# Copying a short filter's result out of PSUM on ScalarE, with the order of a single-core kernel rewritten

## The chip, the cores and the metric

The kernel runs on one core of one Trainium2 chip. The metric is the device time of one execution in microseconds. A core has five engines with a queue each: TensorE (PE, which does the matmuls and writes to PSUM), VectorE (DVE), ScalarE (ACT), GpSimd (POOL) and SyncE (SP, which here only issues DMAs). Each engine executes its own queue strictly in order and waits at an instruction until its inputs are there and its output may be overwritten.

## What is computed

Two long convolutions over a sequence of 2048 positions and 448 channels are mixed with a gate. B stands for the branch with a short shift filter, A for the branch whose kernel comes from a state space model:

```
g = sigmoid((u * gate_w).sum(-1))            # one gate for each position
a = causal_conv(u, K) + u * Dskip            # K from 256 complex modes of each channel
k_shift[t] = sum over 4 taps of k[t - tap] * shift_k[tap]
kv = k_shift * v
b = u * (causal_conv(kv, ssm_k) + kv * ssm_D)
out = g * a + (1 - g) * b
```

The change is at `kv = k_shift * v`, the first thing that branch B needs.

## The kernel before

The 448 channels are worked on in four groups of 112, one for each 32 partitions, and, in time, in four quarters H = 0 to 3 of 28 channels of each group. The list `PLAN` (line 37) names the steps: `T` builds the table of A's kernel for a quarter, `B` and `A` do the convolution of a branch for a quarter, `m` mixes. A convolution spreads its inputs with matmuls (`spread`, line 368), transforms them (`transform`, 380), exchanges halves of the partitions by DMA (`swapped`, 750), multiplies on VectorE (`products`, 426), and goes back by two stages of matmuls (`stage_a`, 397, and `stage_b`, 408). Every result in PSUM must be copied to SBUF by VectorE or ScalarE. A table (`table`, 921) needs exponentials on ScalarE (`exps`, 445), sines (`levels`, 452), a long row of VectorE products (`tables`, 592; three `split`s of each table or half table end in an accumulating DMA issued by GpSimd, line 551) and many small matmuls (`sums`, 632). Quarter 3's table is made in two halves.

Before all that stands a part that is done once: the loads, the constants, the modal part (`Modes.run`, 675: transposes of A, B and C on TensorE, products on VectorE, the copy of B on ScalarE; it fills `hold`, which the exponentials of the first tables read), and the shift filter (line 839). The filter runs over eight blocks of 8 positions of each row; in each, 56 matmuls of k (loaded transposed) with diagonal matrices of the taps (`dg`, 799) fill a PSUM room of 2 x 448 columns, and VectorE multiplies the room with v, in place, in `natv` (line 852).

What sets the order of the work:

- All calls are first recorded and numbered in program order (`Listed`, 112) and then issued in the order of the hand-written list `ORDER` (line 52), which `Order.issue` (132) turns into an order for each engine: each instruction is tied to the one ahead of it on its engine. The profile so shows line 137 for all of them, and they are told apart by tile.
- `SIDES` (45) holds one letter for each copy out of PSUM, phase addition and change of sign (`Sides`, 336): V for VectorE, S for ScalarE.
- `ROOMS` (41) says which of four PSUM rooms (`ps0` to `ps3`) each user takes, `SLOTS` (38) which of seven SBUF buffers (`q0` to `q6`, 3584 columns of bf16) each user takes. The buffers are reused, so a user waits for the one before it. The taps have a buffer of their own call (line 766): their raw form `wr` in the first half, `dg` in the second.

In the trace, `natv` holds v and then kv; `natu` first holds k and then u; `ps` is a PSUM room; `TP` and `TQ` are the table's products; `ET` its exponentials and sines.

Of the kernel before, what the change touches and what calls it, by code (L numbers as in the profile page):

```python
# [38 lines left out]
    "201031456232433120056615532041060303231061540604265013"  # L39
)  # L40
ROOMS = (
    "031230120122130132023010223312031201320001012121201100302332131110331210203301002313130323111031203103303210320132212000"
    "13111112310221033031032020012311212323010303033031323212102022201023121232131202010303130"
)
SIDES = (
    "SVSSSSSVSSSSSSSSSSSSSSSSSSSSSSSVSSSVSSVSSSSSSSSSSSSSSSSSSVVVVVSSSSSSSSSSSSSSSSSSSSSSSSSSSSSSSSSSSSSSSSSSSSSVVVVSSSSSSSSS"
    "SSSSSSSSSSSSSSSSSSSSSSVSSSSSSSSSSSSSSVSVVSVVSSSSSSVSSSSSSSSSSSVSSVVSSSSSSSSSVSVSVSSSVSSS"
)
ORDER = (
# [643 lines left out]
def body(  # L693
# [21 lines left out]
    V = nc.vector  # L715
# [120 lines left out]
    kg = KGen(nc, places, cons, ar, arena, sel_d, d4, hold, evac)  # L836
    nc.gpsimd.memset(shaped(arena["TQ"][:], [32, 2 * M])[:, 31], 0.0)

    for b0 in range(0, 64, 8):
        pt = places.room()  # L840
        for i in range(2):
            for d in (0, -1, 1, -2, 2, -3, 3):
# [170 lines left out]
```

## Time and profile before

| | |
|---|---|
| three timed executions | 260.49, 262.22, 262.29 us (median 262.22) |
| span of the profiled execution (a time of its own beside the span is not on its page) | 257.9 us |
| mean granted clock of TensorE | 0.929 |
| instructions on TensorE, VectorE, ScalarE | 5631, 378, 278 |
| idle time of VectorE behind its last instruction | 10.3 us |

The page's first part gives the busy time of each engine; a view by stretches gives the same between two times, in the order PE, PE's weight loads, DVE, ACT, POOL. The view of waits says who waited for whom: total, times, longest. A group by form is `line engine op out<-in shapes xcount | busy us, mean ns | idle before us`. Instructions of VectorE and ScalarE that follow each other overlap by some 0.08 to 0.15 us in the records, so the time from start to start is a little under the mean.

### The profile page before, as it was taken

The page shows a single profiled execution, that of the slowest core. Times are in us where ns is not written, and L with a number is a line of the kernel's source. Part 1 is how long each engine was busy: PE and PEld are TensorE (multiplying, and loading weights), DVE is VectorE, ACT ScalarE, POOL GpSimd, SP SyncE. Part 2 cuts the span into 40 slices and gives each one's busy share as a digit, 9 for nine tenths or more (in the row PEclk, how much of TensorE's full clock was granted, in tenths as well). Part 3 has the DMA queues.
Part 4 walks back from the last instruction along what each step waited for, and adds up shares of the span by engine and source line. Part 5 has one row for each costly group of instructions (what it writes and reads, how often), then busy time and mean ns, then how long its engine had stood idle before and what let it go on. Part 6 is the DMA issues. An engine that isn't in the chain of part 4 may idle for free.

```text
span 257.9 us, 12431 instructions
## 1 busy us (share of the span) xinstructions
PE 208.9 (81%) x5631; PEld 188.6 (73%) x5631; DVE 237.4 (92%) x378; ACT 199.5 (77%) x278; POOL 30.5 (12%) x81
## 2 busy tenths in 40 slices
PE   0634784988779999998889998989999998999820
PEld 0511484978669898997879887888899897998810
DVE  4999999999999999999999999988999999998830
ACT  2299993089979999999999999989999975653300
POOL 8970001200000002100000021000031120000000
PEclk9995596899979999999999999997999999999975
DMA  6999983499861347475043055600462375120088
GB/s 167 212 164 216 165 178 74 82 171 159 139 157 32 47 106 144 79 167 91 7 99 104 3 102 95 149 24 3 111 110 38 57 145 131 29 51 4 3 163 125
DMA packets 58917, 26.44 MB, mean 103 GB/s; under 512 B 49520, under 2 KB 57200, under 8 KB 58864
## 3 DMA queue, kind: packets, MB, share of 16 engines
q1 hardware_dynamic: 52192, 18.65, 39.5%
q0 software_dynamic: 2160, 5.51, 12.2%
q10 hardware_dynamic: 4512, 1.49, 3.0%
q8 instruction: 44, 0.72, 1.2%
q14 instruction: 9, 0.07, 0.1%
HBM read 8.17 MB, written 2.52 MB: 41 GB/s over the span
## 4 chain that ended last, share of the span: by engine, by line
DVE 61%; PE 17%; issue 6%; DMA 5%; ACT 5%; SPq 1%; POOL 1%; DVEq 0%; ACTq 0%; POOLq 0%
DVE TP L137 18%; PE ps L137 17%; DVE q L137 15%; DVE TQ L137 15%; DVE natv L137 5%; ACT q L137 3%; DMA TP<-TP 3%; DVE ET L137 3%; DVE G L137 2%; DVE RK L137 1%; SPq L137 1%; DMA q<-q 1%; ACT ET L137 1%; DMA sk<-in_B_ssm_k_dram 1%; DVE hold L137 1%
## 5 line engine op out<-in xcount | busy, mean ns | idle before, releaser
L137 ACT CAST q<-ps 128x1024 bf16<-128x1024 f32 (+4 forms) x151 | 126.6, 929 | 23.9 <-PE ps L137 23.1
L137 PEld LDWEIGHTS <-q 128*128 128x128 bf16 (+2 forms) x720 | 52.3, 147 | 13.5 <-DMA q<-in_A_A_re_dram 8.4
L137 DVE TENSOR_TENSOR TQ<-TQ,ET 128x896 bf16<-128x896 bf16 (+2 forms) x70 | 45.5, 687 | 0.1
L137 PEld LDWEIGHTS <-natu 128*32 128x32 bf16 (+1 forms) x560 | 30.6, 183 | 8.9 <-issue 7.2
L137 PE MATMUL ps<-TP,TQ 128*32 128x32 bf16 x1792 | 33.3, 240 | 4.1 <-DVE TQ L137 2.6
L137 PE MATMUL ps<-q,s_W 128*128 128x112 bf16 (+1 forms) x544 | 33.8, 214 | 3.5 <-ACT q L137 3.4
L137 PE MATMUL ps<-sa_R,q 128*128 128x128 bf16 x448 | 33.3, 229 | 2.4 <-DVE q L137 1.0
L137 PEld LDWEIGHTS <-TQ 128*32 128x32 bf16 x1792 | 30.1, 153 | 6.7 <-DVE TQ L137 3.1
L137 DVE TENSOR_TENSOR q<-q,q 128x3584 bf16<-128x3584 bf16 (+1 forms) x22 | 32.4, 1513 | 1.2 <-ACT q L137 1.2
L137 PEld LDWEIGHTS <-s_W 128*128 128x128 bf16 x544 | 28.2, 100 | 6.5 <-issue 4.5
L137 DVE TENSOR_TENSOR TP<-TP,ET 128x1792 bf16<-128x1792 bf16 (+3 forms) x25 | 31.4, 1275 | 0.1
L137 POOL DMA_DIRECT2D TP<-TP x15 | 13.1, 914 | 153.8 <-PE ps L137 89.6
L137 PEld LDWEIGHTS <-G 128*128 128x128 bf16 x1024 | 27.9, 96 | 4.3 <-issue 2.5
L137 PE MATMUL ps<-q,G 128*128 128x28 bf16 x1024 | 28.5, 175 | 1.4 <-ACT q L137 1.4
L137 ACT ACTIVATE q<-hold 128x224 bf16<-128x224 f32 x64 | 22.4, 414 | 5.0 <-DVE hold L137 5.0
L137 PE MATMUL ps<-q,natu 128*32 128x336 bf16 (+3 forms) x336 | 17.8, 334 | 5.7 <-DVE natv L137 4.2
L137 ACT ACTIVATE ET<-q 128x1344 bf16<-128x1344 int16 (+1 forms) x12 | 17.2, 1457 | 1.4 <-DVE q L137 1.3
L137 PE MATMUL ps<-q,q 128*32 128x336 bf16 (+3 forms) x112 | 17.8, 334 | 0.0
L137 PE MATMUL ps<-Wc,natu 128*64 128x128 bf16 x224 | 15.5, 285 | 0.6 <-DVE q L137 0.6
L137 ACT CAST RK<-ps 128x448 bf16<-128x448 f32 (+1 forms) x16 | 11.5, 742 | 5.4 <-PE ps L137 5.4
L137 DVE TENSOR_TENSOR TQ<-TQ 128x448 bf16<-128x448 bf16 (+2 forms) x35 | 15.3, 446 | 0.1
L137 DVE CAST q<-ps 128x1024 bf16<-128x1024 f32 (+3 forms) x13 | 12.6, 978 | 2.4 <-PE ps L137 1.4
(81 smaller groups left out, 276.6 us busy)
## 6 DMA issues: line engine op xcount, KB each, us to landing
q<-q SPq DMA_DIRECT2D x64, 112.0 KB, 3.1
TP<-TP POOLq DMA_DIRECT2D x9, 448.0 KB, 5.0
natv<-in_B_v_dram SPq DMA_DIRECT2D x4, 448.0 KB, 7.3
sk<-in_B_ssm_k_dram SPq DMA_DIRECT2D x16, 112.0 KB, 3.8
natu<-in_A_u_dram SPq DMA_DIRECT2D x4, 448.0 KB, 10.2
TP<-TP POOLq DMA_DIRECT2D x6, 224.0 KB, 3.8
out_dram<-natv SPq DMA_DIRECT2D x8, 112.0 KB, 4.6
out_dram<-natv ACTq DMA_DIRECT2D x8, 112.0 KB, 4.5
```

The source lines that it names most:

```text
L137: ins = f(*args, **kw)
```

## The change

1. In the filter, ScalarE (by the new letters in `SIDES`, S for all eight) copies each block from PSUM to SBUF in bf16, and VectorE's product with v reads that copy. The copies use two buffers in turn, each of 2 x 448 columns, in the half of the taps' buffer that held `wr`, which is spent once `dg` is built. The blocks are recorded in the order 16, 48, 8, 24, 32, 0, 40, 56.
2. `SLOTS`, `ROOMS`, `SIDES` and `ORDER` are written anew. The instructions are otherwise the same.

```
-    for b0 in range(0, 64, 8):
+    for i0, b0 in enumerate((16, 48, 8, 24, 32, 0, 40, 56)):
         pt = places.room()
...
         o = vt[:, b0:b0 + 8].rearrange("p (i b) l -> p i (b l)", i=2)
-        V.tensor_tensor(out=o, in0=pt[:, :, 0:448], in1=o, op=ALU.mult)
+        f = shaped(taps, [2, 448], at=896 * (i0 % 2))
+        evac(f, pt[:, :, 0:448])
+        V.tensor_tensor(out=o, in0=f, in1=o, op=ALU.mult)
```
```
 SLOTS = (
-    "201031456232433120056615532041060303231061540604265013"
+    "020260153465641042231116123354602264421130151001205634"
 )
```

The lists `ROOMS`, `SIDES` and `ORDER` are long strings; what the new ones say, read off by laying the recorded calls of both kernels beside each other:

- Beside the eight new copies on ScalarE, twelve things change sides. To ScalarE go three 1024-wide copies out of PSUM, one 896-wide, one 512-wide, one 448-wide, the 64-wide copy of the gate's sums and one 672-wide phase addition; to VectorE go three 896-wide phase additions and one 448-wide copy. VectorE then has 374 instructions and ScalarE 290 with its DMA issues left out.
- `SLOTS` puts the taps into buffer 0, in which A_re, A_im and B_re were loaded first (before, they had buffer 1 for themselves). The DMA that loads them moves from the first place of ScalarE's queue to the 18th, behind twelve exponentials and the copy of B.
- The two instructions that build `dg` were VectorE's 17th and 22nd and are its 69th and 64th.
- VectorE's first half of `hold` was its 36th instruction and is its 31st. The product for the half that is held back (`xfd`), which stood ahead of it, stands behind it.
- On GpSimd the partition index `c_pidx` comes first, and the four longest fills come behind some forty short ones; before, a long fill came first.
- On SP the four transposed loads of k come ahead of the four loads of v; before, one load of v stood between them.
- Ahead of the first copy of a spread, ScalarE's queue holds 60 instructions where it held 46: added are the eight filter copies, seven exponentials of the second table and one change of sign; one exponential and one phase addition move behind it.
- VectorE's 99th instruction is the last product with v in both orders; ahead of it, seven products and sums of the first table's `TQ` now take the place of two of its three splits, four phases of the second table and a change of sign.
- The steps of the convolutions and tables behind that keep their sequence by and large, and are interleaved anew.

More of the change, by code (lines that the diff above doesn't have):

```diff
@@ L38 @@
 SLOTS = (
-    "201031456232433120056615532041060303231061540604265013"
+    "020260153465641042231116123354602264421130151001205634"
 )
 ROOMS = (
-    "031230120122130132023010223312031201320001012121201100302332131110331210203301002313130323111031203103303210320132212000"
-    "13111112310221033031032020012311212323010303033031323212102022201023121232131202010303130"
+    "02131320012123120310303112130210300312021332031302013210231213011301130113201301221330221123000013133021310132220223"
+    "210023220032132301310012023231122032123303232020211313032101330302333110201302112031131230223"
 )
 SIDES = (
-    "SVSSSSSVSSSSSSSSSSSSSSSSSSSSSSSVSSSVSSVSSSSSSSSSSSSSSSSSSVVVVVSSSSSSSSSSSSSSSSSSSSSSSSSSSSSSSSSSSSSSSSSSSSSVVVVSSSSSSSSS"
-    "SSSSSSSSSSSSSSSSSSSSSSVSSSSSSSSSSSSSSVSVVSVVSSSSSSVSSSSSSSSSSSVSSVVSSSSSSSSSVSVSVSSSVSSS"
+    "SSSSSSSSSSSSSSSSSSSSSSSSSSSSSSSSSSSSSSSSSSSSSVSSSSSSSSSSSSSSSSSSVVVVVVVSSSSSSSSSSSSSSSSSSSSSSSSSSSSSSSSSSSSSSSSSSSVV"
+    "VVVVSSSSSSSSSSSSSSSSSSSSSSSSSSSSSSSSSSSSSVSSSSSSSSVVSSVVSSSSSSVSSSSSSSSSSSSSSSSVSSSSSSSSSVSSSSSVSSVS"
 )
 ORDER = (
[54 rows of a table removed]
[54 rows of a table added]
 )
```

108 rows, old and new, of the table ORDER are left out of this document.

## The prediction

> **What bounds the kernel now.** I read the page's busy shares first, then the busy time of each engine in six stretches, then the waits of ScalarE and TensorE, then single groups by form and stretches of the timeline.
>
> ```profile
> span 257.9 us, 12431 instructions
> PE 208.9 (81%) x5631; PEld 188.6 (73%) x5631; DVE 237.4 (92%) x378; ACT 199.5 (77%) x278; POOL 30.5 (12%) x81
> ```
> ```profile
> 0.00:13.45 13.45, 4.75 (x48) 4.09 (x48) 10.01 (x37) 3.40 (x4) 12.21 (x36) 1.00 0.93 185
> 13.45:40.73 27.28, 15.14 (x240) 9.86 (x241) 27.04 (x49) 27.22 (x44) 4.60 (x29) 0.74 1.08 169
> 40.73:52.48 11.75, 10.26 (x256) 9.23 (x256) 11.75 (x13) 0.09 (x1) 2.74 (x3) 0.73 0.53 100
> 52.48:204.28 151.80, 138.95 (x3799) 129.25 (x3800) 148.44 (x222) 146.60 (x201) 9.25 (x12) 0.98 0.49 91
> 204.28:247.60 43.32, 39.76 (x1292) 36.17 (x1290) 40.09 (x61) 22.20 (x31) 1.72 (x2) 1.00 0.30 64
> 247.60:257.90 10.30, 0.00 (x0) 0.00 (x0) 0.04 (x1) 0.00 (x0) 0.00 (x0) 0.54 0.88 145
> ```
>
> The columns of the second fence are the stretch, its length, and busy time (count) of PE, PE weight loads, DVE, ACT and POOL, then the TensorE clock, the DMA share and GB/s. VectorE (DVE) carries 237.4 of 257.9 us, and of its 20.5 us without work 10.3 lie behind its last instruction, where only stores run. But the share is an average. From 13.45 to 40.73 both VectorE and ScalarE are full. From 40.73 to 52.48 VectorE is full and ScalarE does nothing (0.09 of 11.75). From 52.48 to 204.28 all three are nearly full: of 151.80 us VectorE lacks 3.36, ScalarE 5.20, TensorE 12.85. After that ScalarE has room and VectorE and TensorE (40.1 and 39.8 of 43.3) share the bound.
>
> ```profile
> ACT q L137 <- PE ps L137: 23.1, 14, 11.7
> ACT q L137 <- DVE hold L137: 5.0, 1, 5.0
> PE ps L137 <- DVE natv L137: 5.2, 3, 4.2
> ```
> ```profile
> 40.89 2.08 DVE L137 TENSOR_TENSOR natv<-ps,natv 128x896 bf16<-128x896 f32 x2
> ...
> 52.93 1.08 DVE L137 TENSOR_TENSOR natv<-ps,natv 128x896 bf16<-128x896 f32 x1
> 53.93 0.61 DVE L137 TENSOR_TENSOR TQ<-TQ,ET 128x896 bf16<-128x896 bf16 x1
> ```
>
> The hole in ScalarE has a cause that can be read off: TensorE waited 4.2 us in one piece for a VectorE product to give back a PSUM room, and ScalarE waited 11.7 us for TensorE. The eight products of the filter with v sit in VectorE's queue between 40.9 and 53.9, and nothing of the first convolution can be spread before the rooms are free.
>
> **The change, part by part.** Durations are means by form from the same execution.
>
> ```profile
> L137 DVE TENSOR_TENSOR natv<-ps,natv 128x896 bf16<-128x896 f32 x8 | 8.4, 1079 | 0.0
> L137 DVE TENSOR_TENSOR TQ<-TQ,ET 128x896 bf16<-128x896 bf16 x36 | 21.7, 621 | 0.1
> L137 DVE CAST q<-ps 128x1024 bf16<-128x1024 f32 x6 | 7.3, 1222 | 2.1 <-PE ps L137 1.1 <-ACT ET L137 1.0
> L137 DVE CAST q<-ps 128x896 bf16<-128x896 f32 x2 | 2.2, 1080 | 0.0
> L137 DVE CAST q<-ps 128x512 bf16<-128x512 f32 x2 | 1.4, 691 | 0.3 <-PE ps L137 0.3
> L137 DVE TENSOR_SCALAR q<-q 128x672 int32<-128x672 int32 x6 | 3.5, 592 | 0.1
> L137 DVE COPY gx<-ps 128x64 f32<-128x64 f32 x1 | 0.2, 221 | 0.0
> L137 ACT CAST q<-ps 128x1024 bf16<-128x1024 f32 x64 | 64.0, 1044 | 16.6 <-PE ps L137 16.2 <-DVE TP L137 0.3
> L137 ACT CAST q<-ps 128x512 bf16<-128x512 f32 x20 | 12.4, 622 | 0.6 <-PE ps L137 0.4
> L137 ACT CAST q<-ps 128x896 bf16<-128x896 f32 x58 | 51.9, 951 | 4.3 <-PE ps L137 4.2
> L137 ACT ACTIVATE q<-q,quarter 128x896 int32<-128x896 int32 x4 | 4.2, 1057 | 0.0
> ```
>
> (1) The product. It read PSUM (1079 ns); now both inputs are bf16 in SBUF, the form of the second row (621 ns). That is 8 x 0.458 = 3.66 us off VectorE.
>
> (2) The new letters for who copies. VectorE loses three 1024-wide copies (3.67), one 896-wide (1.08), one 512-wide (0.69) and the small gate copy (0.22). Two 448-wide copies cancel. It gains three 896-wide phase additions and loses one 672-wide: no row shows the 896 form on VectorE, so it is bounded by 592 ns below and by 592 x 896/672 = 789 above; I take 789, since its ns grow with size, which makes 3 x 0.789 - 0.592 = +1.78. VectorE's sum is -3.66 - 3.67 - 1.08 - 0.69 - 0.22 + 1.78 = -7.5 us.
>
> (3) ScalarE gains the eight filter copies, 8 x 0.951 = 7.6, three 1024-wide (3.1), one 896 (0.95), one 512 (0.62), and gives away the three additions (3.2): some 10 us of means. In a row the copies follow each other faster, as the next fence shows: two 896-wide copies start at 68.27 and the next instruction at 69.86, so 0.80 each.
>
> ```profile
> 13.45 0.67 ACT L137 ACTIVATE q<-hold 128x224 bf16<-128x224 f32 x2 [4.98 <-DVE hold L137]
> 15.56 2.90 ACT L137 ACTIVATE q<-hold 128x224 bf16<-128x224 f32 x10
> 52.48 4.94 ACT L137 CAST q<-ps 128x1024 bf16<-128x1024 f32 x5 [11.67 <-PE ps L137]
> 68.27 1.84 ACT L137 CAST q<-ps 128x896 bf16<-128x896 f32 x2
> 69.86 0.54 ACT L137 ACTIVATE q<-hold 128x224 bf16<-128x224 f32 x1
> ```
>
> (4) Does ScalarE reach the first spread copy later? Ahead of it stood 46 instructions, now 60. What is added is eight copies (8 x 0.80 = 6.4), seven exponentials of the second table (10 take 2.90, so 2.0) and a sign change; an addition and an exponential go behind it: +8.0 us net. It used to have all that done by 40.73 and then stood until 52.48. It also starts earlier: its first exponential waited until 13.45 for VectorE's first half of `hold`, which was VectorE's 36th instruction and is now its 31st, ahead of the products for the tables held back, and GpSimd's partition index, the first thing VectorE waits for, is now GpSimd's first instruction and no longer behind a long iota.
>
> ```profile
> 0.84 2.00 POOL TP L137
> ```
> ```profile
> 10.50 1.87 DVE L137 TENSOR_SCALAR one<-TP 128x32 bf16<-128x32 int32 x1
> 12.81 0.61 DVE L137 TENSOR_TENSOR hold<-ps,TP 128x448 f32<-128x448 bf16 x1
> ```
>
> That iota took 2.00 us. Against it, long GpSimd fills now come later, and VectorE stood in one of them (an instruction of 32 columns took 1.87 us at 10.50). I take 2 us earlier, between 0 and 3. The two buffers cost something: copy n+2 waits for product n, and by the order this makes ScalarE wait about 0.8 us in all. So the first spread copy comes at 40.73 + 8.0 - 2.0 + 0.8 = 47.5 instead of 52.48, 5.0 us earlier. VectorE passes the last filter product earlier too: the same number of instructions (99) now holds 4.1 us less work by their own records, so 49.8 for 53.93. TensorE finishes the filter when the copies let it, some 5 us earlier.
>
> (5) From there to the last copy of the second A convolution (204.28) ScalarE has 2.6 us more work than before (added up in the same way, 10.6 more up to that point, 8.0 of them already done). With the waits it had, 5.20 us, it comes there at 204.28 - 5.0 + 2.6 = 201.9, a gain of 2.4. VectorE, with its old waits, gains its whole 7.5. TensorE's work is unchanged; it starts 5 us earlier and has 12.85 us of waits, so it does not forbid 7.5. The gain lies between 2.4 and 7.5. Waits in this stretch are mutual, and an engine that would be 2.6 us late uses up part of its 5.20 us of waits; I take about the middle, 4.8.
>
> (6) Moves that I cost at nothing. The shift taps now live in the buffer of A_re, A_im and B_re, so their load leaves ScalarE's queue not at its start but behind twelve exponentials and the copy of B: 11.45 + 12 x 0.29 + 1.6 = 16.5 us. The taps are first read by VectorE's 64th instruction; the 63 ahead of it hold 24.1 us by their own records, and with the 3 us that VectorE stood before them that is 27. VectorE's modal part so covers the load for 10 us; cover gone, each us is a us of the end. On SP the four transposed loads of k now stand ahead of all loads of v, which is the same issue work in another order: the last load of v leaves near 27, as before (21.80 + 5.14 below), and v is first used past 40. The loads of u, at SP, wait for the filter's last matmul, which comes earlier. On GpSimd the accumulating DMAs keep their places behind VectorE's splits; the tightest, in the last table, has 5.2 us from split to use.
>
> ```profile
> 21.80 5.14 SPq L137 DMA_DIRECT2D natv<-in_B_v_dram x3
> ```
> ```profile
> L137 POOL DMA_DIRECT2D TP<-TP x15 | 13.1, 914 | 153.8 <-PE ps L137 89.6
> ```
> ```profile
> TP<-TP POOLq DMA_DIRECT2D x6, 224.0 KB, 3.8
> natv<-in_B_v_dram SPq DMA_DIRECT2D x4, 448.0 KB, 7.3
> q<-in_B_shift_k_dram ACTq DMA_DIRECT2D x1, 448.0 KB, 5.4
> ```
>
> Those accumulating DMAs take 0.9 us to issue and land after 3.8, so 5.2 is enough with little over.
>
> Sum: span 257.9 - 4.8 = 253.1. The timed median, 262.22, lies 4.3 above that span; I keep that distance, so 257.4 us.
>
> **A rule weighed.** In these rows a copy and a product cost 951 + 621 = 1572 ns against 1079. The Trainium skill, "VectorE: DVE Perf Modes", section "Rules for kernel authors", says that an elementwise operation on a matmul's output should either accept the slow rate or be copied to SBUF first if many operations follow; here only one follows, so the rule speaks against this change. By it the sum would be a loss of eight times 0.49 us of engine work; by the rows the two halves are on different engines, and one of them is in an 11.7 us hole. What it would give as a mechanism is rival A.
>
> **Rivals.**
> A. ScalarE becomes the pace and gives it all back. For it: 146.6 of 151.8 us are full and 2.6 are added. Then the earlier start of `hold` does not come (first spread copy at 49.5, 3.0 earlier) and the waits stay: 262.22 - 3.0 + 2.6 = 261.8, no measurable change. Against it: waits of 5.2 us are there to shrink.
> B. The taps land late; this is the one that ends slower. VectorE executes in order, so it stands at its 64th instruction, and filter, copies and spread with it. Break-even is a landing at 27 + 4.8 = 31.8 us; beyond 34.4 it is over 1% slower. For it: the load now falls into the stretch with a DMA share of 1.08, until 40.7 us. The worst I can argue is a landing with the old stretch's last loads, near 36.5: 257.4 + 9.5 = 266.9. Against it: v's loads of the same size in that stretch took 7.3 us, which makes 24. The Trainium skill, "DMA: Bandwidth & Descriptors", has each DMA engine take turns between queues; by that rule a load on ScalarE's own queue does not stand behind SP's and B does not happen, but no row here shows the two at once.
> C. The rewritten order brings waits of its own past 52 us, where three engines are 92 to 98% full. One place decides: the last table's splits. If their DMA needs more than 5.2 us, VectorE and then the last sums wait, in each half of that table; to lose 4.8 + 2.6 us and be 1% slower it must land 3.7 us later both times, 8.9 us behind its split where the rows give 4.7. That gives 264.8 and, at double the rows' 4.7, 266.
> D. All of VectorE's 7.5 us is got: 254.7. This is the good end of the forecast.
>
> **How the numbers follow.** Two runs of this kernel differ by up to 0.7%, so about 1% (2.6 us) is what a measurement can tell from none. Forecast with D (254 to 259.6): 0.60. A and its neighbours (259.6 to 264.8): 0.18. B: 0.11. C: 0.11. So faster 0.60, same 0.18, slower 0.22; the time is the forecast's, 257.4. The forecast's own range is 254.0 to 259.6. For 8 in 10 the range must take in A and half of B and C: 254.0 to 266.0, which leaves out about 0.1 above and 0.1 below.
>
> **What would show it.** VectorE's busy sum near 230 with 374 instructions, the product near 620 ns; ScalarE near 208; ScalarE's first spread copy near 47.5 and no wait above 4 us between 14 and 47 (step 4); VectorE's 64th instruction without idle before it (B wrong) or with a wait for the DMA of B_shift_k (B right); ScalarE's last copy of the second A convolution between 197 and 202 (step 5), or at 204 and later (A); no wait of VectorE for the TP accumulation (C wrong). The prediction is wrong if ScalarE's hole is filled and the end does not move, or if VectorE's idle time grows by more than 7.5 us.

## The result and the profile after

The changed kernel took 259.75 us (median of 19 executions, 257.51 to 261.93), the kernel before, beside it on the same chip, 260.61. The ratio is 0.9932 (95% interval 0.9902 to 0.9961), so 1.8 us were gained, and I had forecast 4.8. (The ratio leaves out executions more than 1.5% above the fastest of their kernel, three of the 19 after and one of the 19 before; with them the two medians lie only 0.9 us apart.) A second measurement of the same two kernels gave 0.9962 (0.9930 to 0.9993), or 1.0 us. The gain is real and small. The time lies inside my range of 254.0 to 266.0, but just outside the forecast's own 254.0 to 259.6, beside rival A's "no measurable change". The profiled execution has a span of 258.0 us against 257.9 before.

The page of the changed kernel, first its busy sums, then the stretches shown above (columns: stretch, length, PE, weight loads, DVE, ACT, POOL, TensorE clock, DMA share, GB/s):

```profile
span 258.0 us, 12418 instructions
PE 205.7 (80%) x5631; PEld 187.0 (72%) x5631; DVE 233.3 (90%) x374; ACT 208.2 (81%) x290; POOL 31.0 (12%) x81
```
```profile
13.45:40.73 27.28, 14.86 (x192) 8.72 (x196) 27.28 (x40) 21.15 (x24) 4.31 (x8) 0.94 1.08 172
40.73:52.48 11.75, 10.45 (x340) 9.99 (x334) 11.75 (x20) 10.67 (x22) 1.50 (x2) 1.00 0.40 76
52.48:204.28 151.80, 137.13 (x3831) 128.90 (x3832) 145.60 (x216) 145.19 (x198) 10.17 (x12) 0.99 0.47 92
204.28:247.60 43.32, 38.27 (x1248) 34.95 (x1237) 38.23 (x60) 22.29 (x30) 2.87 (x4) 0.96 0.33 70
```

ScalarE's hole from 40.73 to 52.48 is filled, as the change meant (0.09 us of work before, 10.67 now). But a new hole has come ahead of it: from 13.45 to 40.73 ScalarE works 21.15 of 27.28 us, where it worked 27.22. The timeline of ScalarE in the changed kernel shows where (the number in brackets is the idle time ahead of the row, and who ended it):

```profile
7.75 3.19 ACT L137 ACTIVATE q<-hold 128x224 bf16<-128x224 f32 x11 [0.81 <-DVE hold L137]
...
17.74 0.86 ACT L137 ACTIVATE q<-q,quarter 128x672 int32<-128x672 int32 x1 [4.71 <-POOL natu L137]
...
37.04 0.91 ACT L137 CAST q<-ps 128x896 bf16<-128x896 f32 x1 [1.74 <-PE ps L137]
...
44.63 1.71 ACT L137 CAST q<-ps 128x896 bf16<-128x896 f32 x2 [0.74 <-DVE natv L137]
46.69 0.91 ACT L137 CAST q<-ps 128x896 bf16<-128x896 f32 x1 [0.34 <-DVE natv L137]
```

ScalarE starts 5.70 us earlier than before (7.75 for 13.45), then stands 4.71 us. The row names GpSimd, but what it waits for is the phases that VectorE makes for it: it starts 0.09 us behind the seventh of eight operations, which ends at 17.65. VectorE's own timeline shows them:

```profile
9.74 0.62 DVE L137 TENSOR_TENSOR hold<-ps,TP 128x448 f32<-128x448 bf16 x1
10.40 7.53 DVE L137 TENSOR_SCALAR q<-hold 128x224 int32<-128x224 f32 x8
17.85 0.60 DVE L137 TENSOR_TENSOR q<-ps,TP 128x448 f32<-128x448 bf16 x1
```

Eight operations on 224 columns, 7.53 us. The group that holds them was cheap before and is not now (kernel before, then the changed one):

```profile
L137 DVE TENSOR_SCALAR q<-hold 128x224 int32<-128x224 f32 x40 | 10.1, 298 | 0.2
```
```profile
L137 DVE TENSOR_SCALAR q<-hold 128x224 int32<-128x224 f32 x40 | 14.8, 421 | 2.8 <-ACT ET L137 2.7
```

The 4.7 us more are busy time, not idle time: VectorE counts as working. Beside it, at those times, GpSimd makes the long fills of the sine tables, which the new order had moved behind some forty short instructions. Two of the fills, and VectorE's operations over the same time, in narrow stretches of the timeline:

```profile
12.29 1.98 POOL L137 IOTA TP<- 32x2048 bf16 x1
14.55 1.81 POOL L137 MEMSET TP<- 32x2048 bf16 x1
```
```profile
11.90 2.50 DVE L137 TENSOR_SCALAR q<-hold 128x224 int32<-128x224 f32 x2
14.33 2.17 DVE L137 TENSOR_SCALAR q<-hold 128x224 int32<-128x224 f32 x2
```

The fills end at 14.27 and 16.36, VectorE's pairs at 14.40 and 16.50: the first pair's second operation (12.30 to 14.40) and the second pair's (14.54 to 16.49) stand until a fill is done. Taken one by one, all eight operations end 0.13 to 0.14 us behind some instruction of GpSimd: three behind a long fill, the others behind short ones of 0.16 to 0.66 us. ScalarE's last filter copy and its first spread copy share a row:

```profile
49.95 1.82 ACT L137 CAST q<-ps 128x896 bf16<-128x896 f32 x2
```

A spread copy takes 1.02 us and the pair ends at 51.77, so the first spread copy comes at 50.75, not at my 47.5. A second new wait lies at 67 us, where ScalarE stands for the gate's matmuls, and these for the load of u (views of waits):

```profile
ACT gx L137 <- PE ps L137: 4.1, 1, 4.1
```
```profile
PE ps L137 <- DMA natu<-in_A_u_dram: 3.1, 1, 3.1
```

### The profile page after: what moved, and what is told of

It is laid out like the page before. It is cut to its first block, busy times and chain, and to the rows that moved or that the text cites. A ratio compares the mean times of both kernels' runs of the same rounds, so it can differ in the third digit from the quotient of the medians.

```text
span 258.0 us, 12418 instructions
## 1 busy us (share of the span) xinstructions
PE 205.7 (80%) x5631; PEld 187.0 (72%) x5631; DVE 233.3 (90%) x374; ACT 208.2 (81%) x290; POOL 31.0 (12%) x81
## 4 chain that ended last, share of the span: by engine, by line
PE 34%; ACT 26%; DVE 17%; DMA 9%; issue 6%; SPq 3%; ACTq 0%; DVEq 0%
PE ps L137 34%; ACT q L137 22%; DVE q L137 6%; DMA natu<-in_A_u_dram 5%; DVE TP L137 5%; SPq L137 3%; DMA q<-in_A_A_re_dram 2%; DMA q<-q 2%; ACT ET L137 2%; DVE G L137 1%; ACT RK L137 1%; DVE ET L137 1%; DVE RK L137 1%; DVE natv L137 1%; ACT L137 1%
## 5 line engine op out<-in xcount | busy, mean ns | idle before, releaser
L137 ACT CAST q<-ps 128x896 bf16<-128x896 f32 (+4 forms) x165 | 137.9, 927 | 18.3 <-PE ps L137 17.0
L137 PEld LDWEIGHTS <-q 128*128 128x128 bf16 (+2 forms) x720 | 51.5, 147 | 14.1 <-issue 6.3
L137 PE MATMUL ps<-q,s_W 128*128 128x112 bf16 (+1 forms) x544 | 32.8, 211 | 6.1 <-ACT q L137 5.4
L137 PEld LDWEIGHTS <-s_W 128*128 128x128 bf16 x544 | 27.4, 98 | 8.5 <-issue 6.8
L137 PEld LDWEIGHTS <-natu 128*32 128x32 bf16 (+1 forms) x560 | 27.9, 181 | 4.8 <-issue 4.4
L137 DVE TENSOR_SCALAR q<-hold 128x224 int32<-128x224 f32 x40 | 14.8, 421 | 2.8 <-ACT ET L137 2.7
L137 PE MATMUL ps<-q,q 128*32 128x336 bf16 (+3 forms) x112 | 15.0, 300 | 2.6 <-DVE q L137 2.6
L137 PE MATMUL ps<-TP 128*128 128x512 bf16 x16 | 7.8, 614 | 10.7 <-POOL TP L137 5.1
L137 PE MATMUL ps<-Wc,natv 128*64 128x128 bf16 x224 | 15.0, 284 | 1.3 <-DVE natv L137 0.9
L137 PE MATMUL ps<-q,natu 128*32 128x336 bf16 (+3 forms) x336 | 15.4, 301 | 0.5 <-DVE q L137 0.4
```

Of the source, the lines that this page charges most:

```text
L137: ins = f(*args, **kw)
```

## The experiments

Two theories stood against each other. The theory of the two waits: the forecast's mechanism holds, and its start was lost first to the fills and then to u. The rival, pace: from 52 us on three nearly full engines set the time, and an earlier start is swallowed. Ratios are to the kernel before, measured beside each. The numbers in the edits are those of the recorded calls.

**The changed kernel again** (no edit).

> The changed kernel once more, unaltered, as the yardstick for the kernels beside it. Both theories: a ratio to the kernel before of about 0.993, ScalarE's first spread copy near 50.75, ScalarE standing some 4 us near 67 for the gate's matmuls.

Measured 0.9962 (0.9930 to 0.9993). It is the yardstick for the next three, which ran beside it.

**The fills moved.** 80 to 83 are the four fills, 110, 112, 113 and 119 phases and a mask, 79 the product that makes `Wc`, 195 a sum of the modal part.

```
 ORDER, the calls of GpSimd alone:
-... 91 118 6 26 ... 18 17 83 21 25 30 28 80 90 81 40 82 89 85 39
+... 91 118 81 83 6 26 ... 18 17 21 25 30 28 90 89 85 80 82 40 39
 ORDER, the calls of VectorE alone:
-... 156 110 119 79 112 113 203 ... 195 199 ...
+... 156 203 ... 195 110 119 79 112 113 199 ...
```

> The four long GpSimd fills of the sine tables (2.0, 2.0, 1.8, 1.8 us) are put elsewhere in GpSimd's order: two where VectorE waits for the first half of hold, two under VectorE's PSUM sums; five short VectorE operations that nobody needs early go behind those sums. Nothing else changes. Theory of the two waits (the early start was lost first to these fills, then to the wait for u): the eight operations that took 7.53 us take about 2.5, VectorE's busy time falls from 233 to about 229, ScalarE's first spread copy comes near 46.5 instead of 50.75, and the end comes 2 to 3.5 us sooner than in the changed kernel: ratio to the kernel before 0.980 to 0.986. Rival (three full engines set the pace from 52 to 204 us and swallow any earlier start): the first spread copy comes just as early, but the end stays within 0.8 us of the changed kernel: ratio 0.990 to 0.996.

Measured 0.9784 (0.9732 to 0.9835), 4.7 us less than the yardstick: the rival's value is outside the interval, and the gain is even a little above the theory's. VectorE, GpSimd and ScalarE in this kernel:

```profile
9.26 1.90 DVE L139 TENSOR_SCALAR q<-hold 128x224 int32<-128x224 f32 x8
...
13.71 3.94 DVE L139 TENSOR_TENSOR TP<-ps,RK 128x1792 f32<-128x1792 bf16 x2
```
```profile
9.53 5.96 POOL L139 IOTA TP<- 128x6 int32 x26
15.53 1.80 POOL L139 MEMSET TP<- 32x2048 bf16 x1
```
```profile
45.41 2.02 ACT L139 CAST q<-ps 128x896 bf16<-128x896 f32 x2 [0.43 <-PE ps L139]
```

The eight operations take 1.90 us for 7.53. The fill at 15.53 now runs wholly under VectorE's two sums from PSUM, and they take 3.94 us, exactly as without a fill beside them in the changed kernel (20.11, 3.94). The first spread copy starts at 46.42: 4.35 us earlier than the yardstick's 50.77. So the shift reached the end in full. The run moves five operations of VectorE too, so the 4.35 us are not those of the eight alone; that the fills are what held the eight is shown by 1.90 for 7.53.

**The gate from v.** The gate's matmuls read v in the place of u, so that nothing there waits for u; the gate that comes out is not the one of the function.

```
-                         rhs=uu[:, :, l], ...
+                         rhs=vt[:, :, l], ...
```

> The gate's 112 matmuls read v in the place of u, so the gate is computed from the wrong tensor, and nothing there waits for the load of u, which is still made. Theory of the two waits: TensorE's 3.1 us for u and ScalarE's 4.1 us for the gate go, the stretch from 64 to 72 us closes up, and the end comes 2 to 4 us sooner than in the changed kernel: ratio 0.978 to 0.986. Rival (pace): the 4 us come back as other waits behind 72 us, ratio 0.990 to 0.996.

Measured 0.9944 (0.9912 to 0.9976): no gain that can be told from the yardstick. Here the theory of the two waits fails in its second half. The wait for u is gone, and two things take its place. VectorE still waits for the next load of the same queue, the second block of `ssm_k` (yardstick, then this kernel):

```profile
71.54 0.29 DVE L137 TENSOR_TENSOR sk<-sk,dB 128x28 bf16<-128x28 bf16 x1 [1.94 <-DMA sk<-in_B_ssm_k_dram]
```
```profile
71.07 0.28 DVE L137 TENSOR_TENSOR sk<-sk,dB 128x28 bf16<-128x28 bf16 x1 [1.47 <-DMA sk<-in_B_ssm_k_dram]
```

And TensorE, which then has the table's sums to do without a pause, stands four times between its own matmuls with nothing that the profile shows to wait for ("issue"):

```profile
75.54 0.32 PE L137 MATMUL ps<-TP,TQ 128*32 128x32 bf16 x7 [1.14 <-issue]
...
79.82 1.22 PE L137 MATMUL ps<-TP,TQ 128*32 128x32 bf16 x63 [0.74 <-issue]
...
83.55 0.33 PE L137 MATMUL ps<-TP,TQ 128*32 128x32 bf16 x7 [0.98 <-issue]
...
87.46 1.15 PE L137 MATMUL ps<-TP,TQ 128*32 128x32 bf16 x57 [0.55 <-issue]
```

That is 3.41 us from 70 to 92; the yardstick has 0.29 there, in one place. TensorE also waits 1.7 us for VectorE's addition on ssm_k there. That these waits are what took the gain back is read from the timeline; no run takes them away. Laid instruction by instruction beside the yardstick, ScalarE is 1.8 us ahead at 80 us and level with it at 88.

**Both together** (the edits of the last two).

> The moved fills and the gate from v together (the gate is again computed from the wrong tensor). Theory of the two waits: the gains add, 4 to 7 us sooner than the changed kernel, ratio 0.966 to 0.978, the first spread copy near 46.5. Rival (pace): ratio 0.988 to 0.995, with the waits of ScalarE and VectorE behind 80 us longer by what the front gained.

Measured 0.9759 (0.9704 to 0.9815): the moved fills' gain, and nothing beyond it that the interval shows. The rival's value is ruled out. The theory's range holds 0.9759 too, but only because the fills alone gave more than it expected; the second gain, which was to be added, is not there.

**The copies undone.** The changed kernel's order, with the product reading PSUM as before the change; `evac.vector()` only passes over the letter in `SIDES`, and the calls are renumbered, since eight fall away.

```
-        f = shaped(taps, [2, 448], at=896 * (i0 % 2))
-        evac(f, pt[:, :, 0:448])
-        V.tensor_tensor(out=o, in0=f, in1=o, op=ALU.mult)
+        evac.vector()
+        V.tensor_tensor(out=o, in0=pt[:, :, 0:448], in1=o, op=ALU.mult)
```

> The changed kernel with its order, but the eight products read PSUM again and the eight ScalarE copies are gone. Theory (the copies carry filter work into ScalarE's hole, and what the first spread copy gains or loses goes through to the end almost whole): VectorE spends 8 x 0.45 = 3.6 us more by its last filter product, ScalarE's first spread copy comes at 53 to 54.5 instead of 50.75, ScalarE's busy time falls by 7.5 us, and the end is 2.5 to 4 us later than in the changed kernel: ratio to the kernel before 1.004 to 1.012. Rival (what the changed kernel gained came from its order alone, and ScalarE is the pace): 7.5 us less work on ScalarE make it no slower than the changed kernel, ratio 0.985 to 0.998.

Measured 1.0148 (1.0101 to 1.0194), some 4.9 us slower than the yardstick by the two ratios (5.7 against 0.9932) and a little more than the theory expected. The first spread copy comes 4.9 us late, more than the products' 3.7 alone; VectorE also waits 2.7 us for the filter's matmuls:

```profile
55.68 1.01 ACT L138 CAST q<-ps 128x1024 bf16<-128x1024 f32 x1 [14.36 <-PE ps L138]
```

So the change of the code is worth about 5 us in this order, which was written for it, and ScalarE, relieved of 6 us, is not the pace.

**Fills moved and copies undone.**

> The moved fills, and the products read PSUM again without the copies. Theory: 2.5 to 4 us later than with the moved fills alone (0.978), ratio 0.988 to 0.995. Rival (ScalarE is the pace): no later than with the moved fills alone, 0.972 to 0.982.

Measured 0.9843 (0.9770 to 0.9916) from executions that scatter over 7 us. It lies between the two and on the edge of both. In its one profile (span 260.5, for 255.5 with the fills moved alone) the first spread copy starts at 51.31 and the two pairs of the table below at 98.99 and 220.34, which is 4.9, 4.7 and 4.6 us later. That is the theory's direction and the size of the run before; by the times, 1.5 us, how much the copies are worth once the fills are moved stays open.

**Three copies back to VectorE**, on top of the moved fills.

```
 SIDES: letters 39, 46 and 150
-S S S
+V V V
```

> The moved fills, and three large PSUM copies given back to VectorE, as the kernel before had them (one 896-wide near 68 us, two 1024-wide near 71 and 164 us): ScalarE is relieved of 2.9 us, VectorE gets 3.5 us more. Theory (neither engine alone sets the pace, their waits are mutual): within 1 us of the moved fills alone, ratio 0.974 to 0.982. Rival A (ScalarE is the pace): 1.5 to 2.9 us sooner, 0.967 to 0.973. The opposite (VectorE is still the pace): 2 to 3.5 us later, 0.986 to 0.992.

Measured 0.9959 (0.9916 to 1.0001): 4.6 us slower than the moved fills alone by the ratios, worse than all three expected and nearest to the opposite (VectorE is still the pace). VectorE now waits at two of the copies:

```profile
67.38 1.09 DVE L139 CAST q<-ps 128x896 bf16<-128x896 f32 x1 [4.66 <-PE ps L139]
```
```profile
165.50 1.23 DVE L139 CAST q<-ps 128x1024 bf16<-128x1024 f32 x1 [2.70 <-PE ps L139]
```

At 67 us VectorE now stands at a copy whose matmuls are behind the gate's, in the wait for u, with all of the tables queued behind it, and 98 us later once more. But these waits stand in the place of others (with the moved fills alone VectorE waits 2.95 us at 67 us for ssm_k). In the two profiles VectorE stands idle for 28.0 us without these copies and 27.8 with them; its busy sum is 2.6 us larger (230.1 for 227.5) and the span 2.4 us longer (257.9 for 255.5). So in the profiles the copies cost what they add to VectorE's work, which speaks for VectorE as the pace. Why the times differ by more stays open.

**Two transforms ahead of the gate's matmuls**, alone and with the moved fills.

```
 ORDER:
-697-760 2044 1629 761-808 1648-1655 1554 872 1630-1637 809 875 1656 ... 1638
+2044 1629 1648-1655 1630-1637 697-808 1554 872 1656 1638 809 875 ...
```

> The changed kernel with the fills where they are, and only the two transforms put ahead of the gate's matmuls on TensorE (their two copies ahead of the gate's copy on ScalarE). Theory (a shift that exists at 88 us is carried unchanged to the end, so what the stretch from 64 to 72 us loses counts): 1.3 to 2.2 us sooner than the changed kernel, ratio to the kernel before 0.986 to 0.992. Rival (as the gate from v suggested, the time comes back as gaps between TensorE's matmuls before 88 us): no gain, ratio 0.992 to 0.997.

> The moved fills, and on TensorE two transforms (with their two copies on ScalarE) ahead of the gate's matmuls, so that ScalarE has 1.6 us of work while u lands. Theory after the gate from v changed nothing (behind u stands the load of the second ssm_k block, and it is this row of loads that holds the stretch): no change, ratio 0.975 to 0.982. Rival (ScalarE's 4.5 us of waiting at the gate are lost at the end): 1.3 to 1.8 us sooner, 0.970 to 0.974.

> The moved fills with the two transforms ahead of the gate once more, unaltered, to compare with the kernels beside it. Both theories: a ratio to the kernel before of 0.970 to 0.977.

Alone: 0.9921 (0.9881 to 0.9962), on the border of the two expectations and not to be told from 0.9932 and 0.9962. With the moved fills: 0.9735 (0.9687 to 0.9783) and, measured once more, 0.9766 (0.9705 to 0.9827), against 0.9784 for the fills alone. What this adds is less than can be told. It is the fastest version measured, 2.3 to 2.7% below the kernel before.

**VectorE's addition on ssm_k later**, on top of that.

```
 ORDER:
-... 879 1853-1869 1905-1912 868 877 ...
+... 879 868 877 1853-1869 1905-1912 ...
```

> The moved fills, the two transforms ahead of the gate, and VectorE's small addition on the second ssm_k block behind a 2.0 us product instead of ahead of it, since VectorE stood 2.4 us there. Theory (VectorE's position past 72 us goes through to the end): VectorE's wait falls from 2.4 to under 1 us, 1 to 2 us sooner than without this move, ratio 0.965 to 0.970. Rival (TensorE and ScalarE wait for u and set the position at 72 us): no change, 0.971 to 0.977.

Measured 0.9804 (0.9738 to 0.9870), no better than 0.9766 beside it: no gain, as the rival said. But the move did not do what the theory needs. In this run's profile VectorE still stands 1.90 us at the addition, now at 70 us, and then 1.65 us at the next copy out of PSUM, so the wait was moved rather than taken away; what it is worth is not shown.

**GpSimd's old order** in the changed kernel.

```
 ORDER, the calls of GpSimd alone:
-1 225 109 223 214 63 75 2 20 ... 83 ... 80 90 81 ... 82 89 85
+81 1 2 5 31 63 225 75 109 15 20 83 6 ... 82 ... 80 ...
```

> The changed kernel with GpSimd's first 55 instructions in the sequence of the kernel before (the long fills at 0.8, 4.3, 6.8 and 10.4 us again, the partition index behind the first); all other engines keep the changed order. Theory of the fills: the first half of hold comes 3 to 5 us later than 7.1, the level operations meet only one fill instead of four, and the first spread copy comes between 48.5 and 51.5; the end within 2 us of the changed kernel, ratio 0.985 to 1.002. Rival (the early partition index is what brought the gain and the late fills cost nothing): the first spread copy at 53 or later and the end 2 us or more later than in the changed kernel, 1.003 or more.

Measured 1.0122 (1.0067 to 1.0177): the rival's case, and I had the size of the first term wrong. The first five rows below are VectorE's, the last is ScalarE's:

```profile
4.40 1.73 DVE L139 TENSOR_SCALAR TP<-TP 128x1 f32<-128x1 int32 x2
...
6.70 1.86 DVE L139 TENSOR_SCALAR TP<-TP 128x32 int32<-128x32 int32 x2 [0.34 <-POOL TP L139]
10.16 2.08 DVE L139 TENSOR_SCALAR gx<-TP 128x128 f32<-128x128 int32 x1 [1.60 <-POOL TP L139]
...
15.29 0.62 DVE L139 TENSOR_TENSOR hold<-ps,TP 128x448 f32<-128x448 bf16 x1 [1.46 <-ACT TP L139]
...
17.76 1.80 DVE L139 TENSOR_SCALAR q<-hold 128x224 int32<-128x224 f32 x8
```
```profile
52.52 2.02 ACT L139 CAST q<-ps 128x896 bf16<-128x896 f32 x2 [0.43 <-PE ps L139]
```

The level operations are quick (1.80 us) because the fills are over, but `hold` comes 8.2 us later than 7.09. The late index is only a part of that (VectorE waits 3.06 us for it at the start, for 1.00 in the changed kernel): three of the fills now stand over VectorE's first small operations, up to 6.13, 8.56 and 12.24 us. So the old place of the fills is not free either, and what the index alone is worth is not shown. Both together: against the old order of GpSimd the new one gains 4 to 5 us (1.0122 against 0.9932 and 0.9962), and with the fills moved nearly 9 (0.9784).

**What carries a shift to the end.** The kernels that differ only ahead of the first spread copy, with that copy's start, the start of the VectorE pair of 3584-wide products near 98 us and of the one near 219 us (rows below for three of them):

| kernel | first spread copy | first pair | second pair | span | span less first copy |
|---|---|---|---|---|---|
| changed, again | 50.77 | 98.39 | 219.43 | 259.6 | 208.8 |
| fills moved | 46.42 | 94.33 | 215.71 | 255.5 | 209.1 |
| copies undone | 55.68 | 104.29 | 225.47 | 265.3 | 209.6 |
| GpSimd's old order | 53.53 | 101.15 | 222.67 | 262.8 | 209.3 |

```profile
98.39 3.95 DVE L137 TENSOR_TENSOR q<-q,q 128x3584 bf16<-128x3584 bf16 x2
...
219.43 3.96 DVE L137 TENSOR_TENSOR q<-q,q 128x3584 bf16<-128x3584 bf16 x2 [0.84 <-ACT q L137]
```
```profile
94.33 3.95 DVE L139 TENSOR_TENSOR q<-q,q 128x3584 bf16<-128x3584 bf16 x2
...
215.71 3.96 DVE L139 TENSOR_TENSOR q<-q,q 128x3584 bf16<-128x3584 bf16 x2 [0.87 <-DMA q<-q]
```
```profile
101.15 3.96 DVE L139 TENSOR_TENSOR q<-q,q 128x3584 bf16<-128x3584 bf16 x2
...
222.67 3.96 DVE L139 TENSOR_TENSOR q<-q,q 128x3584 bf16<-128x3584 bf16 x2 [1.06 <-ACT q L139]
```

The first copies lie 9.3 us apart, and what follows them is 208.8 to 209.6 long. Between the two pairs pass 121.0 to 121.5 us. The last column is the weaker evidence: the fastest version, profiled twice, has 205.7 and 209.8 there, with 120.5 and 122.0 between the pairs, so one kernel alone can differ that much; but no kernel shows a shift worked off. The stretch that I took for three engines with slack to share is rigid: a shift that exists at 98 us is there at 219. VectorE, less its busy time, stands 3.7 to 4.2 us between the pairs in these four kernels (3.2 before the change). The simplest reading is that its full queue carries the shift, which fits the three copies given back; no run was made to tell it from waits that the engines hand to each other.

## Why the prediction was right or wrong

The number came nearer than the sum had earned. The 4.3 us that I kept between span and time set a single profiled execution against a median of others; where one execution has both on record they are 1.7 to 1.8 apart (259.75 beside 258.0). With that the sum would have been 254.9, 4.9 below the time measured, and the kernel before, measured nineteen times, has a median of 260.61 and not 262.22. That 259.75 lies inside the range is in part luck.

Step 1 held: the product takes 631 ns (8, together 4.9 us), for 621 forecast.

Step 2 was too large for the kernel as it ran. VectorE's busy sum fell by 4.1 us to 233.3, not by 7.5 to 230. The difference is less than the 4.7 us that the fills added to the group of 224 columns; with the fills moved the sum is 227.5. The 896-wide additions took 625 ns, between my bounds.

Step 3 held: ScalarE's sum is 208.2, as I said near 208. (The terms that I listed add up to 9.1, not to some 10; it grew by 8.7.)

Step 4 failed: "the first spread copy comes at 40.73 + 8.0 - 2.0 + 0.8 = 47.5". It came at 50.75. With what the rows show in place of my terms the sum closes: the start was 5.70 earlier, not 2.0, and the waits of ScalarE between 14 and 50 us were 4.71 + 1.74 + 0.74 + 0.34 = 7.53, not 0.8, so 40.73 + 8.0 - 5.70 + 7.53 = 50.56. Two terms were mis-sized and partly cancel: the start, 3.7 us better than I took it, and the waits, 6.7 us worse. The waits made the forecast fail. 4.71 us of them are the fills; 1.74 are a wait for the filter's matmuls that I had not foreseen and that is still there (1.48) with the fills moved. I had quoted VectorE standing 1.87 us in a fill, and set it against the earlier start without a size of its own; I did not ask which of VectorE's instructions would run at the times to which the new order moves the fills. They were eight of one kind, one behind the other, on which ScalarE's queue hung. The moved fills show it: 4.35 us at the first copy, 4.7 at the end.

The Trainium skill states this as a rule: "SBUF — State Buffer", section "Who interferes with whom", says that GpSimd shares a pair of ports with VectorE under an exclusive lock, that VectorE's copies and scalar operations between SBUF operands can take the pair, where they meet the conditions of a two-port mode, and operations with one SBUF input beside PSUM do not, and that whichever starts second stands for the whole instruction of the other. The trace agrees in both halves: pairs that end 0.13 and 0.14 us behind a fill, and sums from PSUM that take 3.94 us with and without one. By that rule the eight operations under three fills could have been costed before the run: three fills of 1.8 to 2.0 us make some 5.8, an estimate, and the eight took 5.6 more than with the fills moved. That it is the ports, and not something else that GpSimd's instructions hold, no run here tells apart.

Step 5 (of 5.0 us earlier, 4.8 reach the end) is right in kind, among the kernels of the table: a shift ahead goes through whole. Its premise that VectorE keeps its old waits did not hold. What the new interleaving behind the copy costs against the old one is less sure: in the two profiled executions that part is 207.2 us after and 205.4 before (258.0 - 50.75 and 257.9 - 52.48), 1.8 us longer, near the 2.6 us of work that ScalarE gained and my lower bound; but VectorE's rows put it elsewhere. In these two profiles VectorE works 4.1 us less and stands 4.2 us more (258.0 - 233.3 = 24.7, for 20.5). Of that, 2.4 to 2.5 us lie between the first spread copy and the first pair (3.6 for 1.1), where it now waits 1.7 us for ssm_k, and 2.4 from the start of the second pair to its last instruction (4.6 for 2.2), above all in one wait, where the kernel before has none behind 204 us above 0.64:

```profile
228.36 0.69 DVE L137 CAST q<-ps 128x512 bf16<-128x512 f32 x1 [2.81 <-PE ps L137]
```

All the kernels with the changed order have this wait, of 1.25 to 3.51 us. So the new order did bring waits of its own behind 52 us, as rival C feared, in other places than the one I named. No run takes this one away.

By the timed runs, of 1.7 us earlier 1.0 to 1.8 stayed. One profile of each does not decide between them: the changed kernel's second profile has 208.8 there. ScalarE's last copy of the second A convolution ended at 206.24, which I had named as a sign of rival A, but it is one that VectorE did before; the copy that came last before ends at 204.83 instead of 204.32.

Step 6 held where it could be seen. VectorE built `dg` at 29.30 without idle ahead of it, and with the moved fills at 23.93, so the taps had landed by then, and rival B, which needed a landing behind 31.8, did not happen. No wait of VectorE for the accumulating DMAs stands in the view of waits, so rival C, in the place that I gave it, did not either. The loads of u, which I put at nothing since they leave SP earlier, did leave 1.9 us earlier (49.19 for 51.12) and landed no earlier: the time from issue to landing was 10.2 to 10.3 us before and 7.2 to 14.1 now, beside accumulating DMAs that take up to 10.6. That wait was real, and taking it away alone gained nothing.

Rival A named the right neighbourhood for the wrong reason. ScalarE is not the pace: relieved of the eight copies the kernel is slower (1.0148), and relieved of three others as well (0.9959 for 0.9784). In both runs VectorE got the work, and in both the span of the profile grew by about as much or more (5.7 us for 3.9, 2.4 for 2.6): VectorE, which I let keep its whole gain, is the likelier pace.

The rule that I weighed (the Trainium skill, "VectorE: DVE Perf Modes", "Rules for kernel authors": copy only if many operations follow) would have had the copies cost 3.9 us. In this order, which was written for them, they bring about 5, and they run on an engine that without them stands 14.36 us; the measurement decides against the rule here.

## What to carry to other kernels

Where an order moves long fills of one engine, lay the other engines' instructions over the new times, and ask of each whether it can stand under a fill; busy time that grows without more instructions is the sign. In a hand-written order with several nearly full engines, find the mark behind which the rest is rigid, count what moves that mark, and count the fullest engine's waits in the new order afresh: in the two profiles they took back all that its work had lost. Before a copy is handed to another engine, look at how full that engine is, at what the copy would wait for and at what stands behind it in that queue.

## What the runs showed of the hardware

VectorE's operations from SBUF to SBUF on 224 columns end 0.13 to 0.14 us behind the GpSimd instruction beside them, a fill of 32 x 2048 (1.8 to 2.0 us) or a shorter one, and the profile books that as VectorE's work: 7.53 us for eight, against 1.80 to 1.90 without fills. Sums that read PSUM are not held (3.94 us with a fill beside them and without).

TensorE has gaps of 0.55 to 1.14 us in long rows of small matmuls with no wait that the profile shows, 3.41 us in 22 us with the gate from v and 0.29 in the yardstick. Between 62 and 97 us they come to 2.4 to 3.4 us in the four variants in which TensorE does not wait there for u (the gate from v and the copies undone, each with and without the moved fills), and to 1.1 or less in those in which it does. Their cause stays open; no run here was made for it.
